# Key padding, the expert choice and the state's addition moved between engines in a gated-attention and mixture-of-experts kernel

## The chip, the core and the metric

The kernel runs on one core of a Trainium2 chip. Time is device microseconds of that core for one execution; a kernel's time is the median of several executions. Five engines run their own instruction streams in order and wait for each other by semaphores: TensorE (PE, with its weight loads as PEld), VectorE (DVE), ScalarE (ACT), GpSimd (POOL) and SyncE (SP), which issues most DMAs. Matrix products land in PSUM, which GpSimd cannot read.

## What is computed

For 4 batches and 8 heads of width 48, over 768 tokens, a gated linear attention keeps a 48x48 state per head; its rows then go to the one of 8 experts with the highest gate logit, and the expert's two-layer network gives the output.

```python
f = 1.0 / (1.0 + np.exp(-f_logit))
for t in range(S):
    state = f[:, :, t, :, None] * state + np.einsum('bhd,bhe->bhde', k[:, :, t], v[:, :, t])
    y[:, :, t] = np.einsum('bhd,bhde->bhe', q[:, :, t], state)
# x: y as 3072 rows of 384
expert_idx = np.argmax(x @ w_gate, axis=1)
# rows in order up to the capacity of their expert, then per expert e
h = np.maximum(disp[e] @ w1[e], 0.0)
out[i] = gate_w[i] * (h @ w2[e])[row of i]
```

## The kernel before

Attention runs over 24 chunks of 128 tokens of one batch, 6 chunks a batch, with the 8 heads as 4 pairs (NP). Chunk n's work is spread over several **slots**: slot n is one pass of `slot(n)` (L826), and its code is written out by hand in the order in which each engine gets its instructions; no scheduler moves them. A slot takes some 4.6 to 6.5 us; the 24 slots are followed by the experts' products, 150 to 325 us of the span, which PE fills alone.

On PE a slot holds, in this order: the scaled keys of chunk n turned to token rows (`keys_pe`, L451, into two buffers of the PSUM pool psT), the scores of chunk n+1 (`scores_pe`, L426, two buffers of psA), the padded keys and queries of chunk n+2 transposed (`kq_in`, L366, again two buffers of psT; that pool has two, so L366 can start only when the copies of the turned keys have left them), in odd slots decay gates (`f_in`, L366 into psF), the product of the old state with the queries (`inter`, L468), the new keys' and values' product (`update`, L488, into a psA buffer), in five slots the ranks of chosen rows (`rank_pe`, L675 to L682, where L679 is the first to read the choice), the attention rows of chunk n-1 (`rows_pe`, L543, psA) and the product of scores and values (`values`, L522). Then slot n+1 starts with its L451. The last chunk of a batch (slots 5, 11, 17, 23) has no L451 and no L488; the first (0, 6, 12, 18) no L468.

On ACT a slot copies the turned keys (`keys_out`, tile kn, L457, two copies), the attention output (yT, L534), the scores (AT, L432, two copies), in even slots takes the sigmoid of the gates (pf, L357), in some slots rounds a weight piece (`split_high`, L135), then copies the rows of chunk n-1 (L559) and their gate logits (tile parts, L569), and from slot 7 on (`PAD_ACT`, L78) pads keys and queries of chunk n+3 into tile kqp (`kq_pad`, L409). Before slot 7 GpSimd pads. On DVE: the choice of experts, the scaled keys and queries (kT and qT, L415), the state's sum U (`state`, L502, or L500, a copy, for a batch's first chunk), and two scans over the gates (`decay` L386 into Suf, `decay_back` L400 into Rq). On GpSimd: masks of the scores (L434), the next state S (`carry`, L508, which multiplies U by the decay), then a scatter of one chunk's rows to their experts' places in DRAM (`flush_scatter`, L326, one or two in a slot from slot 7), sums of gate logits (L577, L578) and parts of weight splits (L144).

The choice of experts for a group of chunks runs in three steps: `choose_sum` on GpSimd, `choose_max` (L583 to L586) at the end of that slot on DVE, and in the next slot `choose_first` (L591, L593), whose result, tile tally, the ranks on PE in the same slot read. These are slots 6, 10, 14, 17 and 20. SP's queue, in order: the keys and queries of chunk n+6 (L210), which overwrite what the padding has read and so wait for it, the gates (L216), the values (L205) and weight pieces (L122, L128).

Of the kernel before, what the change touches and what calls it, by code (L numbers as in the profile page):

```python
# [14 lines left out]
AF = mybir.ActivationFunctionType  # L15
ALU = mybir.AluOpType
# [13 lines left out]
def kernel(  # L30
# [12 lines left out]
    nc = tc.nc  # L43
    B, H, S, D = q.shape
# [9 lines left out]
    R = 64 + D  # L54
# [23 lines left out]
    PAD_ACT = 7  # L78
# [54 lines left out]
    def split_high(piece):  # L133
        raw, hi, lo = piece
        return nc.scalar.activation(hi, raw, AF.Copy)  # L135
# [82 lines left out]
    def loaded(nm, n):  # L218
        return loads[nm, n % NLOAD[nm]]
# [16 lines left out]
    Sb = []  # L236
# [115 lines left out]
    def sig(u):  # L352
        if u >= NT // 2:
            return
        cuts = (0, 64, P) if u == 0 else (0, P)
        for r0, r1 in zip(cuts, cuts[1:]):
            pace["ins"] = nc.scalar.activation(  # L357
                pf[u % 2][r0:r1, :, :, :D], loaded("f", u)[r0:r1].rearrange("t h j d -> t j h d"), AF.Sigmoid
            ).ins
# [43 lines left out]
    def kq_pad(n):  # L403
        if n < NT:
            src = loaded("kq", n).rearrange("t h j d -> t j h d")
            if n - 3 < PAD_ACT:
                nc.gpsimd.tensor_copy(kqp[n % 2][:, :, :, :D], src)
            else:
                nc.scalar.activation(kqp[n % 2][:, :, :, :D], src, AF.Copy)  # L409

    def kq_in(n):
        pts = transposes(*((psT.tile([P, NP, C], F32, name="psT"), kqp[n % 2], h) for h in range(2)))
        for nm, pt, by, made in (("kT", pts[0], Sufb[n % 2], kTs), ("qT", pts[1], Rqs.pop(n), qTs)):
            t = abuf.tile([P, NP, C], F32, name=nm, bufs=3)
            nc.vector.tensor_tensor(t[:R].rearrange("r p t -> r (p t)"), pt, by[:R], op=ALU.mult)  # L415
            made[n] = t
# [22 lines left out]
    def first(n):  # L439
        return n % CPB == 0  # L440

    def last(n):
        return n % CPB == CPB - 1
# [10 lines left out]
    def keys_out(n, pks):  # L454
        kn = abuf.tile([P, NP, R], F32, name="kn")
        for s, m in enumerate(MS):
            nc.scalar.activation(kn[:, :, 64 * s : 64 * s + m], pks[s][:, :, :m], AF.Copy)  # L457
        kns[n] = kn
# [37 lines left out]

    def state(n, pu):
        U = abuf.tile([P, NP, D], F32, name="U", bufs=1)
        if first(n):
            nc.vector.tensor_copy(U[:R], pu[:R])  # L500
        else:
            nc.vector.tensor_tensor(U[:R], pu[:R], Sb[n % 2][:R, :, :D], op=ALU.add)  # L502
        pus[n] = U

    def carry(n):
        if n in pus:
            U = pus.pop(n)
            nc.gpsimd.tensor_tensor(  # L508
                Sb[(n + 1) % 2][:R, :, :D],
                U[:R],  # L510
                pendall[:R, n + 1].unsqueeze(2).broadcast_to([R, NP, D]),
                op=ALU.mult,
            )
# [75 lines left out]
    def choose_first(g, m, w):  # L589
        wm = abuf.tile([P, m], F32, name="r_wm")  # L590
        nc.vector.tensor_reduce(out=wm, in_=w, axis=AX.X, op=ALU.max)  # L591
        oh = tallies[-1][:, 1 : m + 1]
        nc.vector.tensor_tensor(oh, w, wm.unsqueeze(2).broadcast_to([P, m, NE]), op=ALU.is_equal)  # L593
        chosen[g] = oh, m
# [171 lines left out]
    quarters, half = [0] * DT, []  # L766
# [59 lines left out]
    def slot(n):  # L826
        slot_now["n"] = n
        prev, cur, nxt = 0 <= n - 1 < NT, 0 <= n < NT, 0 <= n + 1 < NT
        kqn, fn = 0 <= n + 2 < NT, 0 <= n + 3 < NT
        tail = n - 1 >= NT - NCH  # L830
        keyed = cur and not last(n)
        done = ends.get(n - 1)
        if keyed and n:
            keys_out(n, keys_pe(n))
        if prev and not (cur and first(n)):
            y_out(n - 1)
        if nxt:
            pas = scores_pe(n + 1)
        if 0 < n < PAD_ACT:
            kq_pad(n + 3)  # L840
        if n == 3:
            nc.gpsimd.tensor_copy(ring[:, :, DM + NE : W], tokid[:, :RING].unsqueeze(2))
        while half:
            choose_first(*half.pop())
        for g in full:
            choose_sum(*g)
        if n == 1:
            f_in(4)
        if kqn:
            kq_in(n + 2)  # L850
        if n % 2 and fn and n not in (1, 9, 15):
            f_in(n + 3, n + 4)
        if nxt:
            scores_out(n + 1, pas)
        if n == 0:
            sig(2)
        if prev and cur and first(n):
            y_out(n - 1)
        if n % 2 == 0 and n > 0 and fn:
            sig((n + 4) // 2)  # L860
        if n in PIECE_SPLIT:
            split_high(pieces[PIECE_SPLIT.index(n)])
        loads_of(n)
        early_job(n, 0)
        if cur:
            inter(n)
        if n in (9, 15):
            f_in(n + 3, n + 4)
        early_job(n, 1)
        if keyed:  # L870
            pu = update(n)
        if split_at["n"] == n:
            pc = split_pe()
        ranks = [(g, chosen[g][1], rank(g, None)) for g in list(chosen) if not done or g != done[0]]
        if keyed:
            state(n, pu)
        if split_at["n"] == n:
            split_count(pc)
        ranked = [(g, m, pick(*job)) for g, m, job in ranks]
        if tail:  # L880
            for g, m, job in ranked:
                put(*job)
                queue.extend(range(g, g + m))
            ranked = []
        if keyed:
            carry(n)
        if n == 0:
            kq_pad(3)
            load("kq", 6)
        if nxt:  # L890
            for s in range(SCATTERS.get(n, 2)):
                flush_scatter()
        if fn:
            F = decay(n + 3)
        if prev:
            px = rows_pe(n - 1)
            if tail:
                rows_logits(n - 1, px)
                rows_copy(n - 1, px)
                chosen[n - 1] = choose_one(row_at(n - 1), abuf, tallies[-1][:, 1:2]), 1  # L900
            else:
                rows_copy(n - 1, px)
                rows_parts(n - 1, px)
        if fn and n >= PAD_ACT:
            kq_pad(n + 3)
            load("kq", n + 6)
        if n in QUARTERS:
            k, parts = QUARTERS[n]
            for part in range(parts):
                split_low(pieces[k], nc.gpsimd, PARTS, quarters[k])  # L910
                quarters[k] += 1
        if fn:
            decay_back(n + 3, F)
        for g, m, job in ranked:
            put(*job)
            queue.extend(range(g, g + m))
            if g + m == SPLIT:
                split_at["n"] = n + 1
        while full:
            g = full.pop()  # L920
            half.append((*g, choose_max(*g)))
        if prev and done and not tail:
            g, m = done
            if n - 1 >= NT - 2 * NCH:
                sum_parts(g, m)
                chosen[g] = choose(rows_at(g, m), m, abuf, tallies[-1][:, 1 : m + 1]), m
            else:
                full.append(done)
        if cur:
            values(n)  # L930
        if n % 2 == 0 and n and fn:
            load("f", (n + 4) // 2 + 2)
        if n == 1:
            f_in(5)
        if tail:
            early_job(n, 2)
            g, m = done
            place(*rank(g, psT))
            queue.extend(range(g, g + m))
            flush_scatter()  # L940
        else:
            early_job(n, 2)
        for k in pieces:
            if k >= DT and PIECE_SPLIT[k] == n:
                split_low(pieces[k], nc.vector)
        if n == 4:
            nc.gpsimd.tensor_copy(cap, cap_i[:, 0:1])
        if n == NT - 5:
            ins = nc.sync.dma_start(xg0, dispv[0, : T_FIRST[0]].rearrange("(k p) w -> p k w", p=P))
            tc.declare_no_dep(ins.ins, group="late", reason="later tokens of this expert go to rows of their own")  # L950
            after(ins, early_ins[0], "the rows of the early tokens")
        if n == NT - 3:
            checks.append(check_decay())
        if n == NT - 2:
            pc = psT.tile([P, 1], F32, name="psT")
            nc.tensor.matmul(pc, onesb[:R], checks[0][:R], start=True, stop=True)
            nc.vector.tensor_copy(bad_i, pc)
# [533 lines left out]
```

## Time and profile before

| | us |
|---|---|
| time, median of 3 executions | 373.35 (372.59 to 375.57) |
| the profiled execution | 375.17 |
| its span, from first to last instruction | 373.4 |
| PE busy | 362.1 |
| DVE, ACT, POOL busy | 247.8, 223.8, 166.5 |
| mean granted TensorE clock | 0.990 of full speed |

The profile is one execution. A matrix product's start is recorded, its end is modelled, so a busy PE may hide a wait inside a product's recorded time; the distance from one group's start to the next group's start shows it. A wait is named by the work that ended it. Idle time of an engine costs only where the engine that bounds the span waits for it.

### The profile page before, as it was taken

How to read it: one execution, taken by the hardware profiler on the slowest of the kernel's cores; microseconds unless marked ns; L12 is line 12 of the kernel's file. 1: busy time of each engine (PE TensorE's matmuls, PEld its weight loads, DVE VectorE, ACT ScalarE, POOL GpSimd, SP SyncE). 2: the span in 40 equal slices, each digit the busy share in tenths (PEclk: the TensorE clock that was granted, in tenths of full speed). 3: DMA queues.
4: the chain of work that ended last, by engine and by line, in shares of the span. 5: the costliest groups of instructions: out<-in, count | busy, mean ns of one | idle time of the engine just before them, and what ended most of it. 6: DMA issues, size and time to landing. Idle time of an engine off the chain costs nothing.

```text
span 373.4 us, 10082 instructions
## 1 busy us (share of the span) xinstructions
PE 362.1 (97%) x3895; PEld 340.8 (91%) x3895; DVE 247.8 (66%) x533; ACT 223.8 (60%) x458; POOL 166.5 (45%) x275
## 2 busy tenths in 40 slices
PE   8999999999899999999999999999999999999993
PEld 7999898888787889999899999999999999999993
DVE  4898988979687866753676296857757665570300
ACT  3356677877586763255477475759578586583310
POOL 6665556675757675235613702127117244144012
PEclk9999999999899999999999999999999999999997
DMA  8999999999997432476696979799797997721001
GB/s 153 187 177 224 205 207 227 256 214 226 213 227 164 130 114 105 133 237 204 191 239 188 286 196 242 212 187 319 169 204 247 172 208 253 129 94 52 14 23 40
DMA packets 111351, 67.86 MB, mean 182 GB/s; under 512 B 93646, under 2 KB 105844, under 8 KB 111296
## 3 DMA queue, kind: packets, MB, share of 16 engines
q1 hardware_dynamic: 107504, 57.09, 69.1%
q0 software_dynamic: 3520, 9.97, 7.7%
q8 instruction: 32, 0.52, 0.6%
q14 instruction: 23, 0.19, 0.2%
q10 hardware_dynamic: 272, 0.10, 0.1%
HBM read 49.46 MB, written 11.43 MB: 163 GB/s over the span
## 4 chain that ended last, share of the span: by engine, by line
PE 84%; issue 8%; ACT 3%; POOL 2%; DVE 1%; POOLq 1%; ACTq 0%
PE psM L1222 15%; PE psA L754 9%; PE psM L1015 9%; PE psT L754 9%; PE psM L754 7%; PE psA L426 6%; PE psY L522 6%; PE psA L543 5%; PE psT L366 4%; PE psY L468 3%; PE psA L488 3%; PE psT L451 3%; PE psF L366 2%; POOL out_dram L326 2%; PE psA L376 2%
## 5 line engine op out<-in xcount | busy, mean ns | idle before, releaser
L326 POOL DMA_INDIRECT out_dram<-yo,g_ti x30 | 31.3, 1042 | 55.6 <-ACT yo L1019 31.7
L434 POOL TENSOR_SCALAR_AFFINE_SELECT AT<-AT 128x512 f32<-128x512 f32 x48 | 29.4, 637 | 23.3 <-ACT AT L432 23.2
L1015 PE MATMUL psM<-w2h,hh 128*128 128x384 f32 (+2 forms) x112 | 37.5, 340 | 0.0
L1015 PE MATMUL psM<-w2l,hh 128*128 128x384 f32 (+2 forms) x112 | 37.3, 338 | 0.0
L1015 PE MATMUL psM<-w2h,hl 128*128 128x384 f32 (+2 forms) x112 | 37.2, 338 | 0.0
L135 ACT ACTIVATE w2h<-raw 128x768 fp32r<-128x768 f32 x32 | 27.0, 844 | 11.2 <-DMA raw<-in_moe_w_dram 11.2
L1222 PE MATMUL psM<-hh,w2h 128*128 128x440 f32 (+3 forms) x96 | 33.7, 351 | 0.0
L1222 PE MATMUL psM<-hh,w2l 128*128 128x440 f32 (+3 forms) x96 | 33.7, 351 | 0.0
L1222 PE MATMUL psM<-hl,w2h 128*128 128x440 f32 (+3 forms) x96 | 33.6, 350 | 0.0
L144 DVE TENSOR_TENSOR w2l<-raw,w2h 128x768 fp32r<-128x768 f32 x28 | 27.8, 994 | 7.7 <-ACT w2h L135 6.9
L386 DVE TENSOR_TENSOR_SCAN Suf<-psF,direv 112x511 f32<-112x511 f32 x24 | 29.1, 1212 | 4.5 <-PE psF L366 4.5
L432 ACT ACTIVATE AT<-psA 128x512 f32<-128x512 f32 x48 | 26.4, 612 | 8.9 <-PE psA L426 5.6
L1242 POOL COPY yo<-yq 128x384 uint16<-128x384 uint16 (+4 forms) x16 | 11.9, 790 | 40.1 <-DMA yq<-yp 38.2
L426 PE MATMUL psA<-qT,kT 48*128 48x128 f32 x384 | 29.4, 293 | 0.0
L400 DVE TENSOR_TENSOR_SCAN Rq<-psF,d 112x512 f32<-112x512 f32 x24 | 29.4, 1223 | 0.0
L326 POOL DMA_INDIRECT disp<-rows,ri x24 | 24.8, 1034 | 9.5 <-issue 4.3
L144 DVE TENSOR_TENSOR w1l<-raw,w1h 128x1024 fp32r<-128x1024 f32 x21 | 26.5, 1269 | 2.9 <-ACT w1h L135 2.6
L761 DVE SCALAR_TENSOR_TENSOR hl<-psA,hh 128x224 fp32r<-128x224 f32 (+8 forms) x26 | 14.2, 547 | 21.3 <-ACT hh L760 19.3
L559 ACT ACTIVATE rows<-psA 128x384 f32<-128x384 f32 x24 | 11.8, 491 | 26.0 <-PE psA L543 19.6
L522 PE MATMUL psY<-AT,ld_v 128*48 128x128 f32 (+1 forms) x384 | 26.9, 278 | 0.0
L426 PEld LDWEIGHTS psA<-qT,kT 48*128 48x128 f32 x384 | 25.8, 201 | 0.5 <-issue 0.5
L135 ACT ACTIVATE w1h<-raw 128x1024 fp32r<-128x1024 f32 x24 | 24.8, 1060 | 1.9 <-DMA raw<-in_moe_w_dram 1.9
(253 smaller groups left out, 1041.7 us busy)
## 6 DMA issues: line engine op xcount, KB each, us to landing
raw<-in_moe_w_dram SPq DMA_DIRECT2D x24, 512.0 KB
raw<-in_moe_w_dram SPq DMA_DIRECT2D x32, 384.0 KB
ld_kq<-in_k_dram SPq DMA_DIRECT2D x24, 192.0 KB
ld_kq<-in_q_dram SPq DMA_DIRECT2D x24, 192.0 KB
ld_v<-in_v_dram SPq DMA_DIRECT2D x24, 192.0 KB
ld_f<-in_f_logit_dram SPq DMA_DIRECT2D x11, 384.0 KB
xg<-disp SPq DMA_DIRECT2D x6, 589.5 KB
xg<-disp SPq DMA_DIRECT2D x3, 393.0 KB
```

The costliest lines, as they stand in the source:

```text
L135: return nc.scalar.activation(hi, raw, AF.Copy)
L144: engine.tensor_tensor(lo[cs], raw[cs], hi[cs].bitcast(F32), op=ALU.subtract)
L326: ins = nc.gpsimd.indirect_dma_start(out=dst, out_offset=bass.IndirectOffsetOnAxis(ap=idx, axis=0), in_=rows, in_offset=None, bounds_check ...
L386: nc.vector.tensor_tensor_scan(out=_view(Suf[:R], m - 1, [[-1, m]]), data0=_view(F, m, [[-1, m]]), data1=_view(direv[:R], m - 1, [[-1, m]] ...
L400: nc.vector.tensor_tensor_scan(out=Rq[:R], data0=F, data1=d1[:R], initial=0.0, op0=ALU.mult, op1=ALU.max)
L426: nc.tensor.matmul(pas[s][:, p], kTs[n][r, p], qTs[n][r, p], start=True, stop=True)
L432: nc.scalar.activation(AT[:, s], pas[s], AF.Copy)
L434: nc.gpsimd.affine_select(AT[:, s], AT[:, s], pattern=[[0, NP], [1, C]], compare_op=ALU.is_ge, fill=0.0, base=0, channel_multiplier=-1)
L522: nc.tensor.matmul(py[b][64 * g : 64 * g + m, a, :], vt[:, 2 * p + s, :m], AT[:, s, p, :], start=(first(n) and a == 0), stop=(a == NP // 2 ...
L754: nc.tensor.matmul(ph[:, :T], a[:, c, fs], x[:, c, :T], start=(n == 0), stop=(n == 3 * DT - 1))
L1015: nc.tensor.matmul(py[:n], x[:, ks], a[:, ft], start=(ft == 0 and m == 0), stop=(ft == FT - 1 and m == 2))
L1222: nc.tensor.matmul(pys[c][:, :T], a[:, ft, cs], x[:, :T], start=(ft == 0 and n == 0), stop=(ft == FT - 1 and n == 2))
```

## The change

Four edits. From slot 7 the state's product leaves PSUM by a plain copy on ACT, and GpSimd adds the old state in front of the multiplication that it has done so far (for a batch's first chunk there is nothing to add); DVE no longer touches U in these slots. The padding on ACT moves from behind the rows' and logits' copies to the place behind the sigmoid, ahead of the weight rounding, of the new state copy and of the rows. The issue of the loads of chunk n+6 moves with it, so that on SP's queue they now stand ahead of that slot's values and weight pieces. In every slot that has one, `choose_first` moves behind the scaled keys and queries.

```diff
     def state(n, pu):
         U = abuf.tile([P, NP, D], F32, name="U", bufs=1)
-        if first(n):
+        if n >= PAD_ACT:
+            nc.scalar.activation(U[:R], pu[:R], AF.Copy)
+        elif first(n):
             nc.vector.tensor_copy(U[:R], pu[:R])
         else:
             nc.vector.tensor_tensor(U[:R], pu[:R], Sb[n % 2][:R, :, :D], op=ALU.add)
...
             U = pus.pop(n)
+            if n >= PAD_ACT and not first(n):
+                nc.gpsimd.tensor_tensor(U[:R], U[:R], Sb[n % 2][:R, :, :D], op=ALU.add)
             nc.gpsimd.tensor_tensor(
...
-        while half:
-            choose_first(*half.pop())
         for g in full:
             choose_sum(*g)
         if n == 1:
             f_in(4)
         if kqn:
             kq_in(n + 2)
+        while half:
+            choose_first(*half.pop())
...
             sig((n + 4) // 2)
+        if fn and n >= PAD_ACT:
+            kq_pad(n + 3)
+            load("kq", n + 6)
         if n in PIECE_SPLIT:
             split_high(pieces[PIECE_SPLIT.index(n)])
         loads_of(n)
...
-        if fn and n >= PAD_ACT:
-            kq_pad(n + 3)
-            load("kq", n + 6)
         if n in QUARTERS:
```

DVE in slot 10, from the scan in front of the choice, before (r_m, r_w and r_wm are steps of the choice, tally its result):

```order
L400 SCALAR_TENSOR_TENSOR Rq<-psF,d_145 112x512
L583 TENSOR_REDUCE r_m<-rows 128x4
L585 TENSOR_TENSOR r_w<-rows,r_m 128x32
L586 TENSOR_TENSOR r_w<-r_w,desc 128x32
L591 TENSOR_REDUCE r_wm<-r_w 128x4
L593 TENSOR_TENSOR tally<-r_w,r_wm 128x32
L415 TENSOR_TENSOR kT<-psT,Suf_141 112x512
L415 TENSOR_TENSOR qT<-psT,Rq 112x512
L502 TENSOR_TENSOR U<-psA,S_147 112x192
```

The same place of the changed kernel (its line numbers are 2 to 4 higher from L500 on):

```order
L400 SCALAR_TENSOR_TENSOR Rq<-psF,d_145 112x512
L587 TENSOR_REDUCE r_m<-rows 128x4
L589 TENSOR_TENSOR r_w<-rows,r_m 128x32
L590 TENSOR_TENSOR r_w<-r_w,desc 128x32
L415 TENSOR_TENSOR kT<-psT,Suf_141 112x512
L415 TENSOR_TENSOR qT<-psT,Rq 112x512
L595 TENSOR_REDUCE r_wm<-r_w 128x4
L597 TENSOR_TENSOR tally<-r_w,r_wm 128x32
L646 TENSOR_TENSOR r_sel<-psA,tally 128x4x8
```

The last two steps of the choice moved behind kT and qT, and U's addition is gone.

ACT in slot 8, from the output copies to the next slot's copies of the turned keys, before:

```order
L534 ACTIVATE yT<-psY 112x2x128 x2
L432 ACTIVATE AT<-psA 128x512 x2
L357 ACTIVATE pf_118<-ld_f_100 128x16x48
L559 ACTIVATE rows<-psA 128x384
L569 ACTIVATE parts<-psA 128x32
L409 ACTIVATE kqp_124<-ld_kq_105 128x16x48
L457 ACTIVATE kn<-psT 128x4x64
```

The same place of the changed kernel:

```order
L538 ACTIVATE yT<-psY 112x2x128 x2
L432 ACTIVATE AT<-psA 128x512 x2
L357 ACTIVATE pf_118<-ld_f_100 128x16x48
L409 ACTIVATE kqp_124<-ld_kq_105 128x16x48
L500 ACTIVATE U<-psA 112x192
L563 ACTIVATE rows<-psA 128x384
L573 ACTIVATE parts<-psA 128x32
L457 ACTIVATE kn<-psT 128x4x64
```

The padding moved ahead of the rows, and the copy of U came in between.

GpSimd in slot 8, from the masks to the sums of logits, before:

```order
L434 AFFINE_SELECT AT<-AT 128x512 x2
L508 TENSOR_TENSOR S_149<-U,pendall 112x4x48
L326 DMA disp<-rows,ri 32256x393
L577 TENSOR_TENSOR parts<-parts 128x4x16
L578 TENSOR_TENSOR rows<-parts 128x4x8
```

The same place of the changed kernel:

```order
L434 AFFINE_SELECT AT<-AT 128x512 x2
L511 TENSOR_TENSOR U<-U,S_147 112x192
L512 TENSOR_TENSOR S_149<-U,pendall 112x4x48
L326 DMA disp<-rows,ri 32256x393
L581 TENSOR_TENSOR parts<-parts 128x4x16
L582 TENSOR_TENSOR rows<-parts 128x4x8
```

The addition stands between the masks and the multiplication, and the scatter behind both.

## Rows read from the trace of the kernel before

**Rows 1.** The page: busy time, share of the span and instructions of each engine.

```profile
PE 362.1 (97%) x3895; PEld 340.8 (91%) x3895; DVE 247.8 (66%) x533; ACT 223.8 (60%) x458; POOL 166.5 (45%) x275
```

**Rows 2.** Timeline, slots 8 to 9: start, duration, engine, line, tiles, idle before.

```profile
53.84 1.19 POOL L326 DMA_INDIRECT disp<-rows,ri  x1 [0.38 <-issue]
54.22 1.12 PE L426 MATMUL psA<-qT,kT 48*128 48x128 f32 x16
54.49 0.60 ACT L457 ACTIVATE kn<-psT 128x256 f32<-128x256 f32 x2
55.73 0.67 PE L468 MATMUL psY<-qT,S 48*64 48x128 f32 x16
56.46 0.89 ACT L357 ACTIVATE pf<-ld_f 128x768 f32<-128x768 f32 x1
57.12 0.36 DVE L502 TENSOR_TENSOR U<-psA,S 112x192 f32<-112x192 f32 x1
57.56 0.51 POOL L508 TENSOR_TENSOR S<-U,pendall 112x192 f32<-112x192 f32 x1
58.16 0.19 ACT L569 ACTIVATE parts<-psA 128x32 f32<-128x32 f32 x1
58.30 1.01 POOL L326 DMA_INDIRECT disp<-rows,ri  x1 [0.23 <-issue]
60.56 0.67 PE L468 MATMUL psY<-qT,S 48*64 48x128 f32 x16
```

**Rows 3.** Timeline, slot 10, the same columns.

```profile
63.86 1.01 POOL L326 DMA_INDIRECT disp<-rows,ri  x1 [0.22 <-issue]
64.40 1.12 PE L426 MATMUL psA<-qT,kT 48*128 48x128 f32 x16
64.79 1.36 SPq L210 DMA_DIRECT2D ld_kq<-in_k_dram  x1
65.26 0.60 ACT L457 ACTIVATE kn<-psT 128x256 f32<-128x256 f32 x2 [0.60 <-PE psT L451]
65.70 0.88 PE L366 MATMUL psT<-ident,kqp 64*112 64x64 f32 x16 [0.18 <-ACT kn L457]
66.44 0.19 DVE L593 TENSOR_TENSOR tally<-r_w,r_wm 128x32 bf16<-128x32 f32 x1
66.51 0.67 PE L468 MATMUL psY<-qT,S 48*64 48x128 f32 x16
66.57 0.69 DVE L415 TENSOR_TENSOR kT<-psT,Suf 112x512 f32<-112x512 f32 x1
67.18 0.68 DVE L415 TENSOR_TENSOR qT<-psT,Rq 112x512 f32<-112x512 f32 x1
67.77 0.22 PE L679 MATMUL psA<-tally,onesb 128*128 128x24 bf16 x3
```

**Rows 4.** Groups by form, 50 to 132 us: count, busy, mean ns, idle before.

```profile
L409 ACT ACTIVATE kqp<-ld_kq 128x768 f32<-128x768 f32 x14 | 11.9, 847 | 0.0
L559 ACT ACTIVATE rows<-psA 128x384 f32<-128x384 f32 x15 | 7.4, 491 | 14.7 <-PE psA L543 14.5
L457 ACT ACTIVATE kn<-psT 128x256 f32<-128x256 f32 x13 | 5.0, 384 | 3.7 <-PE psT L451 2.7 <-PE psA L426 1.0
L457 ACT ACTIVATE kn<-psT 128x192 f32<-128x192 f32 x13 | 4.3, 328 | 0.1
...
L415 DVE TENSOR_TENSOR kT<-psT,Suf 112x512 f32<-112x512 f32 x15 | 10.4, 691 | 6.3 <-PE psT L366 6.3
```

**Rows 5.** Timeline, slot 6, the columns of rows 2.

```profile
46.04 0.69 DVE L415 TENSOR_TENSOR kT<-psT,Suf 112x512 f32<-112x512 f32 x1
46.96 0.22 PE L679 MATMUL psA<-tally,onesb 128*128 128x24 bf16 x3
```

**Rows 6.** Busy by stretch: PE, PEld, DVE, ACT, POOL, granted clock, DMA share, GB/s.

```profile
96.50:100.00 3.50, 2.54 (x53) 1.77 (x49) 1.91 (x3) 2.86 (x7) 3.42 (x8) 0.99 1.21 216
100.00:103.40 3.40, 3.40 (x45) 3.34 (x41) 2.62 (x5) 1.31 (x3) 2.02 (x4) 0.51 1.07 202
```

## The prediction

> **What bounds the kernel now.** I read the page first. PE is busy for 362.1 us of the span and no other engine is busy for more than 66% [rows 1]. So PE's own row of work is the bound, and of the other engines only what PE waits for counts. Behind slot 23 PE alone is at work, so that whatever a slot gains or loses reaches the end one for one.
>
> The second view is the timeline of single slots, with the question where PE waits. A product's end is modelled, so I go by starts. In slot 8, L426 starts at 54.22 and L468 at 55.73, 1.51 apart [rows 2]. In slot 10 the same two stand at 64.40 and 66.51, 2.11 apart [rows 3]: PE did no more work, and .60 were lost. Between them L366 started "behind ACT kn", and kn itself had waited .60 for L451 [rows 3]. Over slots 8 to 21 the groups by form put this at 2.7 + 1.0 = 3.7 us, all of it on the first of kn's two copies [rows 4]. Nothing stands in front of the padding's own 14 instructions (idle 0.0) and 14.5 us of idle stand in front of the 15 row copies [rows 4]: ACT has room there.
>
> The third is what ran while kn was late. The view names L451, but in slot 10 PE was through L451 when it began L426, at 64.40, ACT was free from 64.66 (65.26 less its idle .60), and kn began only at 65.26, .86 after L426; in slot 8 it began .27 after [rows 2, 3]. A scatter on GpSimd lay across slot 10's gap, from 63.86 to 64.87 [rows 3]. I read this as L451's signal coming late while the scatter runs, .39 after its end. That is an inference, and one row speaks against it: in slot 8 a scatter lay there too, from 53.84 to 55.03, and kn came on time [rows 2]. The change moves the scatter as well as the padding.
>
> The fourth is the busy time by stretch. In 96.5 to 100 us PE is busy for 2.54 of 3.50, and the next 3.4 us run at a granted clock of 0.51, the 1.2 GHz level, although PE is busy in all of them; ahead it was 0.99 [rows 6]. At half speed 3.40 us do the work of 1.7, so this fall costs 1.7 us at most; I take 1.5, since part of it may be waits inside the recorded times. Waits of about 1 us in one stretch thus can cost more than their length.
>
> **The change part by part.** The sum is against the profiled execution, 375.17, which is 1.8 above the median 373.35 of the runs.
>
> *Padding ahead of the rows.* 14 paddings of 847 ns [rows 4] go from behind the logits' copies, in front of the next slot's kn, into the wait of 14.5 us in front of the row copies, about 1.0 each. In that place they cost nothing as long as the row copies do not come later than their products allow. In even slots the sigmoid, .89, stands ahead (slot 8: 56.46 to 57.35 [rows 2]); padding to 58.20, U's copy to 58.53, rows and logits (.49 + .19) to 59.21, where before the logits ended at 58.35 and the padding about 59.2. So kn comes no later, but the logits are copied up to .9 later, which keep a psA buffer from the next L426, 54.22 + about 4.5; I put .2 for seven even slots together. If the cover were gone wholly, each slot would lose up to .85. What is gained: the kn waits, 3.7 us, if all of them go. The bounds are 0 (they come from the scatter, which stays) and 3.7; I count the whole and book separately what comes back.
>
> *Loads of chunk n+6.* Two DMA issues a slot go ahead of the values and weight pieces on SP's queue. No padding waited for its loads (0.0 [rows 4]), which come three slots ahead; values move back by two issues. The slots of 4.6 us and more hide that: 0. If the cover were gone, a slot would wait for its values for what the two issues take on the queue, at 1.36 for the keys [rows 3] some 2.7 us, once.
>
> *U on ACT, the addition on GpSimd.* DVE loses 12 x .36 = 4.3 us [rows 2] that PE did not wait for. ACT gets 14 copies of 112x192 from PSUM, nearest to the 328 ns of kn's 128x192 [rows 4], between that and the .49 of the row copy. GpSimd gets 12 additions; the trace of before has none, so its bounds are the DVE's .36 for the same addition and 1.01, the longest row of GpSimd in that slot; the nearest row is its own multiplication of the same size, .51 [rows 2], which I take. In slot 8 U was ready at 57.48 and S at 58.07, and L468 of slot 9 reads S at 60.56 [rows 2]: 2.5 us of slack. Now U is ready at 58.53, added at 59.1, S at 59.65: .9 is left. On the path: 0. Were the cover gone, each slot would pay what exceeds .9. The Trainium skill (GPSIMD Engine Reference, section 4.1, Engine selection) advises against this: an elementwise addition belongs on VectorE, since GpSimd is about twice as slow with two inputs. Here DVE's .36 against GpSimd's .51 for two inputs is 1.4 times; by the page's factor the estimate would be .72, S .2 later, and the sum the same.
>
> *What comes back: the scatter.* It stands behind the multiplication on GpSimd. Before, it began .23 after it; now the multiplication ends about .5 later in odd slots and 1.6 later in even ones, so in even slots the scatter of 1.01 moves from 58.30 to about 59.9, that is from the start of slot 9's L451 to the time of kn's second copy and L366 behind it. If the scatter holds signals back, the wait is not removed but goes to other slots: I put .4 (its lag behind the scatter's end in slot 10) for slots 8, 14, 16 and 20, 1.6 us; .9 for the two scatters each that stand in slots 18 and 19, which now end later; and .5 in slots 10 and 17, where L366 coming .6 earlier finds DVE still at the scan and the first three steps of the choice, so that kT gains less than L366. Together 3.0; bounds 0 and, with .4 in all 13 slots, 5.2.
>
> *The choice behind kT and qT.* PE never waits for kT by itself; DVE's kT waited 6.3 us for PE's L366 [rows 4]. So kT coming earlier gains nothing. But L679 on PE reads tally. In slot 10 before, kT began at 66.57 and L679 at 67.77, with tally ready at 66.63. Now tally is ready behind kT (.69), qT (.68) and L591 and L593 (.41 from the first one's start to the other's end), with their overlap of .08 taken off: 1.70 after kT's start, 68.27, so .50 late [rows 3]. In slot 6: 46.04 + 1.70 = 47.74 against 46.96, .78 late [rows 5]. Slots 14, 17 and 20 are built as 10. In sum .78 + 4 x .5 = 2.8 us of new PE wait, with rows L543, values L522 and the next slot queued behind it. Bounds: 0 where PE is late anyway, 4.0 with .8 in each.
>
> Sum: -3.7 + 3.0 + 2.8 + .2 = +2.3 us, so 377.5 for an execution like the profiled one, and **375.7** for the median.
>
> **The rivals.** *Faster.* The scatter holds nothing back (it was the padding, or the late place is free of signals), so the kn waits go for good, and with the one in slot 16 the fall of the clock, 1.5. Then -3.7 - 1.5 + 2.8 + .2 = -2.2: **371**; and 368 if the choice is hidden too, at its bound of 0. For it: the scatter of slot 8 that delayed nothing. Against it: in slot 10 ACT had been free for .60 when kn began, so that the padding was not what it waited for. Chance .25, of which .15 ends beyond 1%.
>
> *The clock falls more often.* The new waits for tally of .5 to .8 fall in slots that have a scatter besides; one stretch with 1.0 idle in 3.5 was followed by 3.4 us at 1.2 GHz [rows 6]. Two more falls at 1.6 give 375.7 + 3.2 = **379**. For it: slots 10, 14 and 17 may then have two waits each. Against it: waits of 3.7 us were there before [rows 4], and the mean granted clock of 0.990 over 373.4 us leaves room for a loss of 3.7 us in all, some two falls. It decides from two more on. Chance .23.
>
> *S comes late.* If the addition takes over 1.4 instead of .51, the slack of .9 is spent, and L468 waits in 12 slots; with the ACT copy late too, .3 each: 375.7 + 3.6 = **379**. For it: GpSimd now does two operations and a scatter in a row. Against it: GpSimd is busy for 45% only [rows 1]. Chance .10.
>
> **How the numbers follow.** The forecast, .42: its own range is 374 to 377.5. The faster rival .25, the clock .23, S late .10. About 1% of the time, 3.7 us, is what a measurement of this kernel can tell from no change, so faster means below 369.6 and slower above 377.1. Faster: .15 from its rival. Slower: .20 of the clock's .23, .08 of S late's .10 and .06 from the upper end of the forecast, .34 together. The rest, .51, is the same. The range runs from 369.0, between the two ends of the faster rival, to 380.0, one more us than both slower rivals; I leave about .10 out on either side.
>
> **What would show it.** Right, in the profile of after: a gap of .5 to .8 ahead of L679's group in slots 6, 10, 14, 17 and 20, with tally (DVE) as what ended it; no wait ahead of kn's first copy anywhere, but a wait of some .4 ahead of the second, or of L366, in even slots, with a scatter lying across it; S ready ahead of L468 everywhere; GpSimd's additions at .4 to .7; row copies without idle time in front in even slots. Wrong: L679 not waiting (then the choice was free, and 2.8 go); no waits with the scatter in its late place (then the padding was the cause, and 3.0 go); a granted clock of .5 in a stretch of slots 6 to 20 in which before had .99, which is the second rival; L468 waiting for S; or weight pieces landing late behind the moved loads.

## The result, and the profile after

| | before | changed |
|---|---|---|
| time, median | 374.10 us (4 executions) | 379.01 us (378.12 to 381.11, 4 executions) |
| ratio | | 1.0139, 95% interval 1.0101 to 1.0177 |
| the profiled execution, its span | 375.17, 373.4 | 381.11, 379.4 |

The change costs 1.4%, some 5 us. In a later measurement of the same two kernels, with 35 and 12 executions, the medians were 373.47 and 375.33 and the ratio 1.0077 (1.0044 to 1.0111). (Ratios leave out executions over 1.5% above the fastest of their kernel and are not the quotient of the medians, which take all.) Together: about 1% slower, with 375.7 forecast and 380 the upper end of the range.

The page of the changed kernel, busy time of each engine (before: [rows 1]):

```profile
PE 357.3 (94%) x3895; PEld 335.4 (88%) x3895; DVE 245.9 (65%) x519; ACT 228.8 (60%) x472; POOL 176.4 (46%) x287
```

PE does the same 3895 products, but stands idle more. What PE waited for between 40 and 200 us, in the table of waits of the changed kernel (total us, times, longest):

```profile
PE psA L683 <- DVE tally L597: 3.9, 5, 1.0
PE psA L758 <- DVE hl L765: 2.0, 1, 2.0
PE psF L366 <- issue: 1.6, 2, 1.0
...
PE psT L366 <- issue: 0.9, 1, 0.9
```

The same table of before has no row above 1.2 us. The new first row is the moved choice: L683 (L679 in before) waits for the tally in all five slots that have one. Slot 6 in the timeline of the changed kernel (start, us, engine, line, tiles, idle before); before stands in [rows 5]:

```profile
46.31 0.69 DVE L415 TENSOR_TENSOR kT<-psT,Suf 112x512 f32<-112x512 f32 x1 [0.37 <-PE psT L366]
...
47.09 1.23 POOL L434 TENSOR_SCALAR_AFFINE_SELECT AT<-AT 128x512 f32<-128x512 f32 x2
...
47.73 0.62 DVE L597 TENSOR_TENSOR tally<-r_w,r_wm 128x32 bf16<-128x32 f32 x1
...
48.41 0.22 PE L683 MATMUL psA<-tally,onesb 128*128 128x24 bf16 x3 [1.02 <-DVE tally L597]
```

And slot 10, to be laid beside [rows 3]:

```profile
67.29 1.12 PE L426 MATMUL psA<-qT,kT 48*128 48x128 f32 x16
67.40 1.01 POOL L326 DMA_INDIRECT disp<-rows,ri  x1 [0.22 <-issue]
67.56 0.60 ACT L457 ACTIVATE kn<-psT 128x256 f32<-128x256 f32 x2 [0.73 <-PE psT L451]
...
68.25 0.62 PE L366 MATMUL psT<-ident,kqp 64*112 64x64 f32 x16
...
68.96 0.69 DVE L415 TENSOR_TENSOR kT<-psT,Suf 112x512 f32<-112x512 f32 x1 [0.82 <-PE psT L366]
...
70.37 0.33 DVE L597 TENSOR_TENSOR tally<-r_w,r_wm 128x32 bf16<-128x32 f32 x1
...
70.76 0.22 PE L683 MATMUL psA<-tally,onesb 128*128 128x24 bf16 x3 [0.53 <-DVE tally L597]
```

kn now starts .27 after L426, as in slot 8 of before, instead of .86: the wait that the change took away is gone. ACT's .73 in front of kn costs nothing, for the padding that filled it has moved. But PE loses at L683 what it won at L366. By starts, L683 comes 1.18, .68, .67, .93 and 1.19 us later behind the rank product ahead of it than L679 does in before, in slots 6, 10, 14, 17 and 20: 4.65 in all. (The expectations below have .70, .90, .70 and 1.27 for the last four.)

The row on hl, the low part of an expert's hidden rows, which DVE makes, is a stretch behind the attention. Busy times there (us of the stretch; PE, PEld, DVE, ACT, POOL; granted clock; DMA share; GB/s):

```profile
190.00:192.30 2.30, 0.32 (x3) 0.13 (x2) 1.08 (x6) 1.94 (x4) 1.59 (x2) 1.00 0.96 375
192.30:196.00 3.70, 3.70 (x10) 3.10 (x11) 3.67 (x8) 3.62 (x8) 0.11 (x1) 0.54 1.13 278
```

PE stands for 2.0 us and then runs most of 3.7 us at a granted clock of .54, near the 1.2 GHz level. Of the 6.0 us between the two profiled spans, by the starts of L426, .3 lie ahead of slot 6, 2.3 between slots 6 and 22 and 3.5 behind. Whether this stall belongs to the change is asked below.

### The profile page after: what moved, and what is told of

Read it like the earlier page. It is cut to its first block, busy times and chain, and to the rows that moved or that the text cites. A ratio compares the mean times of both kernels' runs of the same rounds, so it can differ in the third digit from the quotient of the medians.

```text
span 379.4 us, 10089 instructions
## 1 busy us (share of the span) xinstructions
PE 357.3 (94%) x3895; PEld 335.4 (88%) x3895; DVE 245.9 (65%) x519; ACT 228.8 (60%) x472; POOL 176.4 (46%) x287
## 4 chain that ended last, share of the span: by engine, by line
PE 72%; issue 9%; DMA 6%; POOL 4%; SPq 3%; DVE 3%; ACT 2%; POOLq 1%; ACTq 0%; DVEq 0%
PE psM L1226 14%; PE psA L758 9%; PE psM L1019 9%; PE psT L758 8%; PE psM L758 6%; PE psA L426 5%; DMA ld_kq<-in_q_dram 5%; PE psA L547 4%; PE psY L526 4%; PE psY L468 2%; PE psT L366 2%; POOL out_dram L326 2%; PE psA L488 2%; PE psF L758 2%; PE psT L451 2%
## 5 line engine op out<-in xcount | busy, mean ns | idle before, releaser
L1246 POOL COPY yo<-yq 128x384 uint16<-128x384 uint16 (+4 forms) x16 | 12.7, 839 | 39.4 <-DMA yq<-yp 37.8
L426 PE MATMUL psA<-qT,kT 48*128 48x128 f32 x384 | 28.4, 281 | 0.7 <-ACT parts L573 0.7
L526 PE MATMUL psY<-AT,ld_v 128*48 128x128 f32 (+1 forms) x384 | 26.1, 273 | 0.0
L426 PEld LDWEIGHTS psA<-qT,kT 48*128 48x128 f32 x384 | 24.7, 189 | 1.5 <-ACT parts L573 1.1
L415 DVE TENSOR_TENSOR kT<-psT,Suf 112x512 f32<-112x512 f32 x24 | 16.5, 688 | 14.2 <-PE psT L366 13.4
```

The source lines that it names most:

```text
L426: nc.tensor.matmul(pas[s][:, p], kTs[n][r, p], qTs[n][r, p], start=True, stop=True)
L526: nc.tensor.matmul(py[b][64 * g : 64 * g + m, a, :], vt[:, 2 * p + s, :m], AT[:, s, p, :], start=(first(n) and a == 0), stop=(a == NP // 2 ...
```

## The experiments

The first four ran on one chip with 29 executions of before (median 374.41), the next four later on the same chip with 35 (373.47), the last four on another chip with 26 (374.97). Each is compared with its own group.

**The choice alone.** The kernel before, with one edit:

```diff
-        while half:
-            choose_first(*half.pop())
...
             kq_in(n + 2)
+        while half:
+            choose_first(*half.pop())
```

> The kernel before with one edit only: choose_first behind kT and qT. Theory (the choice carries the loss): in the profile of after PE stands for tally in slots 6, 10, 14, 17 and 20, and the distance between the two kernels grows there by 1.18, .70, .90, .70 and 1.27, so this edit alone costs 4.7 us: about 378.8 against 374.1. Rival (the loss is the late state and scatter, and the wait for tally only takes the place of waits that come anyway): 375 to 376.

Measured: 379.03, ratio 1.0106 (1.0058 to 1.0155). This edit alone costs as much as the whole change. PE's waits in its profile, 40 to 200 us:

```profile
PE psA L679 <- DVE tally L593: 2.9, 5, 1.0
...
PE psT L366 <- ACT kn L457: 0.6, 3, 0.3
```

kn's waits stayed, since neither padding nor scatter moved. In slot 20 the wait for the tally was also followed by a fall of the clock, in the busy times by stretch (the columns are those of the stretch on hl):

```profile
124.00:126.50 2.50, 1.98 (x39) 1.81 (x41) 2.08 (x7) 1.10 (x2) 1.64 (x4) 0.91 0.21 34
126.50:130.00 3.50, 3.50 (x44) 3.15 (x42) 3.16 (x7) 2.35 (x7) 1.54 (x4) 0.58 0.53 149
```

So waits of 2.9 us grew to more: by starts, PE fell back 3.6 us at L679 and another 1.4 between slot 20's L522 and slot 21's L366. That the wait of slot 20 caused the fall is not shown: the longer one of slot 6 (1.0) had none behind it.

**The padding alone.** `kq_pad(n + 3)` and `load("kq", n + 6)` behind the sigmoid, nothing else.

> The kernel before with one edit only: the padding and the loads of chunk n+6 ahead of the rows. Theory (a scatter on GpSimd holds the signal for kn back, and this edit does not move the scatter): kn's waits of 3.7 us stay, 374 as before. Rival (the padding was what made kn late): they go, 370, or 369 with the clock's fall in slot 16.

Measured: 375.62, ratio 1.0026 (.9995 to 1.0057): no gain. kn's lateness stayed. Slot 14 in its timeline:

```profile
88.50 1.01 POOL L326 DMA_INDIRECT disp<-rows,ri  x1 [0.22 <-issue]
...
88.75 0.46 PE L451 MATMUL psT<-ident,kT 64*128 64x64 f32 x8
...
89.88 0.60 ACT L457 ACTIVATE kn<-psT 128x256 f32<-128x256 f32 x2 [1.31 <-PE psT L451]
...
90.32 0.88 PE L366 MATMUL psT<-ident,kqp 64*112 64x64 f32 x16 [0.17 <-ACT kn L457]
```

ACT stood free for 1.31 us, with the padding long done, and kn still began only .37 after the scatter's end. The padding was not the cause. New was a wait of L488 for its values, .67 and a further .62 in slot 10, after which the granted clock was .53 from 71 to 74.5 us.

**The state alone.** U by ACT, the addition by GpSimd, nothing else.

> The kernel before with one edit only: U copied on ACT and the old state added on GpSimd. Theory (the scatter holds signals back wherever it lies): the scatter comes .5 to .9 later, kn's waits of 3.7 us shrink but a wait ahead of L366 of about .4 to 1.0 comes in some slots; 373 to 375. Rival (S or U late is what costs): L468 waits for S, or L488 for the psA buffer that U leaves, in most slots, 377 or more.

Measured: 372.50, ratio .9939 (.9911 to .9967). It is the only one of all kernels here, the changed one included, whose interval lies below 1. Slot 14 in its timeline:

```profile
85.05 0.46 PE L451 MATMUL psT<-ident,kT 64*128 64x64 f32 x8
...
85.44 1.01 POOL L326 DMA_INDIRECT disp<-rows,ri  x1 [0.22 <-issue]
85.55 0.60 ACT L457 ACTIVATE kn<-psT 128x256 f32<-128x256 f32 x2
...
86.30 0.61 PE L366 MATMUL psT<-ident,kqp 64*112 64x64 f32 x16
```

The same place of before:

```profile
84.05 1.01 POOL L326 DMA_INDIRECT disp<-rows,ri  x1 [0.22 <-issue]
84.30 0.46 PE L451 MATMUL psT<-ident,kT 64*128 64x64 f32 x8
...
85.48 0.61 ACT L457 ACTIVATE kn<-psT 128x256 f32<-128x256 f32 x2 [0.63 <-PE psT L451]
```

GpSimd's addition has pushed the scatter from .25 ahead of L451 to .39 behind it, and kn starts .50 after L451 instead of 1.18. The scatter runs in both when L451 ends, but L451's modelled end falls .07 behind the scatter's start instead of .70. All of kn's idle time between 50 and 132 us was .7 us, against 3.7 [rows 4], and it stood in slot 7, which has no scatter ahead of it; in slots 8 to 22 there was none. The waits at L366 that the theory expected in exchange did not come, but for one of .6 on DVE's Rq.

**Padding and state, the choice in its old place.**

> The changed kernel with choose_first back in its old place. Theory (the choice carries the loss): 379.0 less 4.7, 374.3, with no wait for tally. Rival (late state and scatter): 377 or more, with waits of about 1.0 at L366 in slots 8, 9 and 19 as in after.

Measured: 373.94, ratio .9997 (.9967 to 1.0027). The changed kernel without the choice's move is as fast as before, as the theory had it. The waits at L366 in slots 8 and 9 were not there, the one in slot 19 was, 1.0.

**The scatter ahead of the multiplication**, in the kernel before:

```diff
+        if nxt:
+            for s in range(SCATTERS.get(n, 2)):
+                flush_scatter()
         if keyed:
             carry(n)
-        if nxt:
-            for s in range(SCATTERS.get(n, 2)):
-                flush_scatter()
```

> The kernel before with one edit: the scatter stands ahead of the state's multiplication on GpSimd instead of behind it, some .7 earlier; padding, U and choice as before. Theory (a scatter that lies across L451 holds kn's signal back; the state's move helped alone because it pushed the scatter past it): kn's waits of 3.7 us go, and with them the clock's fall in slot 16, so 371 to 372 against 374.4. Rival (the state's move helped because U is taken off DVE or comes at another time): kn's waits stay, 374.4; S comes later by the scatter's 1.0 and has 2.5 of slack.

Measured: median 372.12, but a ratio of 1.0014 (.9981 to 1.0047): no difference that can be told, where the theory had 2 to 3 us. The waits did go as foretold. The group of kn in its profile (50 to 132 us: count, busy, mean ns, idle before):

```profile
L457 ACT ACTIVATE kn<-psT 128x256 f32<-128x256 f32 x13 | 5.0, 382 | 0.0
```

From 3.7 to 0.0, with only the scatter moved. In this profile slot 6's L426 to slot 22's took 80.95 us, against 86.21 in before, of which the fall of the clock in slot 16 is at most 1.7 [rows 6]; what is left, 3.5 or more, fits kn's waits. Behind slot 22 PE lost 1.69 at 183 us to the stall on hl.

**The loads back.** Padding and state, but the loads of chunk n+6 issued at the slot's end.

> Padding and state moved, choice in its old place, but the loads of chunk n+6 issued at the slot's end as before instead of ahead of the values. Theory (the loads' new place makes the values late: L488 waited .7 and .6 for ld_v in slot 10 with the padding moved alone, .5 with padding and state): no such wait, 372.5, like the state moved alone. Rival (the padding in its new place costs, by pushing U, the rows and the logits back): 374, as with the loads moved.

Measured: 373.12, ratio 1.0032 (.9986 to 1.0078), not to be told from the kernel with the loads moved (.9997), so that it decides for neither expectation. The wait for values was gone from the profile, and others stood there: L547 .7 and L426 .5.

**The changed kernel again.**

> The changed kernel once more, unaltered. The stall of 2.3 us at 190 us in its first profile, with the rows' load of the next expert late, is counted to the change by one reading: then it stands in this profile too. By the other it is the chance of one execution, as the weight loads land: then it is missing or smaller, and the time of this profile is 377 to 379 instead of 381.1. Median 378.7 to 379 by both.

Measured: 375.33, ratio 1.0077 (1.0044 to 1.0111). PE's waits in this profile, 40 to 200 us:

```profile
PE psA L683 <- DVE tally L597: 2.1, 4, 0.8
PE psA L488 <- DMA ld_v<-in_v_dram: 1.8, 2, 1.2
PE psF L366 <- DVE Rq L400: 1.0, 1, 1.0
```

The stall on hl is missing, so it is no part of the change. It stood in the profiles of seven of the twelve experiments, of padding alone and of the early scatter among them, at 1.0 to 2.5 us. The median fell below what both readings had said; the first measurement's other three executions (378.1 to 379.1) have no trace, and why they were slower stays open. The waits for the values came in addition here.

**The ranks behind the rows**, in the changed kernel, so that PE works while the tally is made:

```diff
-        ranks = [(g, chosen[g][1], rank(g, None)) for g in list(chosen) if not done or g != done[0]]
...
                 rows_parts(n - 1, px)
+                ranked = [(g, m, pick(*job)) for g, m, job in [(g, chosen[g][1], rank(g, None)) for g in due]]
```

> The changed kernel with the ranks on PE moved behind the products of the rows (L547), so that PE has .76 us of other work while the tally is made. Theory (the choice costs what PE stands for the tally): of the waits 1.2, .7, .7, .7 and 1.2 only .4 each in slots 6 and 20 are left, the loss shrinks by 3.8, 375.2 against 379.0. Rival (the choice's new place costs in another way, by pushing DVE's later work, the scans and the copy of U's buffer): 378 to 379 as before, with the wait for the tally gone all the same.

Measured: 374.68, ratio 1.0083 (1.0045 to 1.0120), as the changed kernel in the same group. The rival was right about the time. The wait for the tally had gone, and this stood in its place:

```profile
PE psA L679 <- ACT U L500: 1.6, 3, 0.6
```

The ranks take the PSUM buffer that U leaves, and U's copy on ACT, behind the padding, is late: one wait turned into another.

**The choice between kT and qT**, in the kernel before, ahead of qT's product inside `kq_in`.

> The kernel before with choose_first moved behind kT only, ahead of qT. Theory (the choice costs only what the tally comes later than PE reads it): the tally is ready .69 + .41 = 1.10 after kT's start, PE read it 1.20 after it in slot 10 and .92 in slot 6, so .0 to .2 a slot, at most .5 in sum: the same time as before within .5. Rival (each step that the choice moves down the queue costs, by what stands behind it on DVE): about half of what the move behind both cost alone (4.6), 2.3 more than before.

Measured: 375.65 against 374.97, ratio 1.0041 (1.0018 to 1.0065). PE waited .7 us for the tally in two slots instead of 2.9 in five. The cost sits between the two expectations, nearer to the theory in the waits; the rest of the .4% no row accounts for. The tally took .26 to .64 us in this kernel, not the .19 of the expectation.

**State and early scatter together**, in the kernel before.

> The kernel before with the state's edit alone and the scatter ahead of GpSimd's addition. Theory (both edits did one thing, to take the scatter off L451's signal): no more than either alone, 1 to 2 us below before, with no wait for kn left. Rival (the state's edit has a gain of its own, DVE without U): 3 us below before.

Measured: 375.94 against 374.97, ratio 1.0024 (1.0003 to 1.0046). Both were wrong. Slot 8 on GpSimd and ACT:

```profile
52.95 1.20 POOL L326 DMA_INDIRECT disp<-rows,ri  x1 [0.20 <-issue]
...
54.31 0.49 ACT L563 ACTIVATE rows<-psA 128x384 f32<-128x384 f32 x1 [1.05 <-PE psA L547]
...
54.77 0.84 ACT L409 ACTIVATE kqp<-ld_kq 128x768 f32<-128x768 f32 x1
...
55.51 0.61 ACT L457 ACTIVATE kn<-psT 128x256 f32<-128x256 f32 x2
```

The scatter now lies across the products of the rows, the row copy begins .16 after the scatter's end, the padding stands behind it on ACT, and kn behind the padding, 1.17 after L451. Which signal the scatter holds is a matter of its place, and here the late one reaches kn through ACT's queue.

**The changed kernel with the early scatter.**

> The changed kernel with the scatter ahead of GpSimd's addition instead of behind the multiplication. Theory (the scatter in its later place holds PE back at L366, .9 to 1.0 in slots 8 and 19): these go, 2 less than the changed kernel, that is 1 to 2 above before, with the waits for the tally left. Rival (those waits are not the scatter's): as the changed kernel, 3 to 4 above before.

Measured: 378.55 against 374.97, ratio 1.0098 (1.0070 to 1.0125): the rival's time. The waits on L366 marked "issue" were gone, as the theory said, but the waits for the tally came to 4.1, 2.6 of it in slot 17:

```profile
103.11 0.51 POOL L512 TENSOR_TENSOR S<-U,pendall 112x192 f32<-112x192 f32 x1
103.12 1.83 DVE L590 TENSOR_TENSOR r_w<-r_w,desc 128x24 f32<-128x24 f32 x1
...
103.56 0.18 POOL L562 COPY rows<-tokid 128x1 f32<-128x1 f32 x1
...
103.70 1.22 POOL L434 TENSOR_SCALAR_AFFINE_SELECT AT<-AT 128x512 f32<-128x512 f32 x2
...
107.07 0.19 PE L683 MATMUL psA<-tally,onesb 128*128 128x16 bf16 x2 [2.59 <-DVE tally L597]
```

A DVE instruction of the choice that takes .19 (median of its five) took 1.83 here: GpSimd worked without a gap from 103.11 to 104.92, and the DVE instruction ended at 104.95.

**Plain work in the scatter's old place**: the early scatter, and eight memsets on GpSimd where it had stood.

> The kernel of the early scatter with eight small memsets on GpSimd (of a spare tile, about 1 us in all) where the scatter stood before, behind the multiplication. Theory (it is the scatter's own making of descriptors that holds signals back, not GpSimd being busy): kn's wait stays 0.0 as with the early scatter alone, and the time 1 to 2 below before. Rival (any work of GpSimd across L451 does it, by its order or its use of memory): the waits of about 3.7 us return, and the time is that of before.

Measured: 377.73 against 374.97, ratio 1.0069 (1.0044 to 1.0094); 2.6 us of PE's waits were now in front of L468, which reads S. (The view names a memset, but S stands ahead of the memsets on GpSimd, behind the early scatters.) The time answers neither side. A slot in which only the memsets lie across L451 does:

```profile
94.48 0.46 PE L451 MATMUL psT<-ident,kT 64*128 64x64 f32 x8
...
94.65 1.35 POOL L893 MEMSET spare<- 128x24 f32 x8
...
95.04 0.60 ACT L457 ACTIVATE kn<-psT 128x256 f32<-128x256 f32 x2
```

kn came on time, .56 after L451, and so it did in slot 21, the other one in which only memsets lie there and ACT was free. GpSimd being busy does not hold the signal back. The 0.0 of the theory did not come back: kn was late by .61, .51, .44 and 1.18 us in slots 13, 14, 19 and 22, where a scatter again ran when L451 ended.

## Why the prediction was right in its main step, and where its terms were off

**kn's waits, -3.7.** Right in the cause, with a limit that the prediction did not see; the price is borne out by starts, not by the times. Of 182 first copies of kn in slots 8 to 22 of the fourteen profiles, 88 had a scatter running when L451 ended (by its modelled end), and 33 of them began over .15 us later than L451 and ACT allowed; of the other 94 one did. So a scatter is needed, whether the padding moved (padding alone: late) or not (early scatter and state alone: none late), and plain work does not do it. But it is not enough, and slot 8 was no lone exception: in before, kn was on time under a scatter in slots 8, 9, 20 and 22 and late in 10, 13, 14, 15, 16 and 19. What counts is where in the scatter L451 ends: within .6 us of the scatter's start 5 of 44 were late, all in kernels with the early scatter, later in it 28 of 44. In the changed kernel a scatter still ran there in seven slots, begun only .03 to .56 earlier, and kn was on time in all. Between .69 and .98 both outcomes occur; what decides there stays open.

As time, the state alone gained .6%, 2.3 us, and the early scatter nothing that can be told, with all 3.7 gone in both. One step of the first paragraph failed here: "Behind slot 23 PE alone is at work, so that whatever a slot gains or loses reaches the end one for one." From slot 22's L426 to the end the fourteen profiles took 241.8 to 246.2 us, and in nine of them PE stood there for hl, .2 to 2.5 us. That spread is as large as the whole change, so a gain of 3 us in the slots can be lost to it.

**The choice, +2.8.** The step that decided, with the right sign and cause, and rather undersized. The waits were 2.9 in the choice alone, 3.9 and 2.1 in the two profiles of the changed kernel; as time the edit cost 1.06%, 4.0 us, with 2.2 to 5.8 as its interval, in which 2.8 still lies; in its profiled execution 1.4 was the clock. The term that was mis-sized is the tally's own .19, taken from [rows 3], where GpSimd was idle. Behind kT and qT it falls under GpSimd's masks and took .18 to .62 (median .33) in the first profile of the changed kernel, .18 to .45 (median .21) in the second, which also had the smaller waits. In slot 6 of the first it began at 47.73 and ended at 48.35, .03 after the mask that ran beside it; slots 10 and 14 show the same. The Trainium skill (GPSIMD Engine Reference, section 1, Specifications) says that GpSimd's paths to SBUF are shared with VectorE, with contention for VectorE instructions that have two SBUF inputs; the tally and L590 have two, kT and qT take one of theirs from PSUM and stay at .69 and .68. These rows agree.

**What comes back, +3.0.** The place was wrong, and the size is measured only together with kn's waits and the row copies: -3.7 + 3.0 + .2 = -.5 was forecast, and padding and state together came to -.1 us (-1.2 to 1.0). The later scatter did not hold up kn's second copy: in the changed kernel kn was on time in every slot. L366 waited .86 in slot 8 with a scatter across it, in one of the two profiles of the changed kernel only. What did come back is U's lateness. In slot 18 of the changed kernel:

```profile
112.93 0.86 ACT L409 ACTIVATE kqp<-ld_kq 128x768 f32<-128x768 f32 x1
...
113.66 0.35 ACT L500 ACTIVATE U<-psA 112x192 f32<-112x192 f32 x1
...
114.05 0.16 DVE L670 TENSOR_SCALAR csplit<-psA 128x1 f32<-128x1 f32 x1 [1.67 <-ACT U L500]
...
117.15 0.66 PE L366 MATMUL psF<-ident,pf 64*112 64x64 f32 x15 [1.01 <-issue]
```

U, behind sigmoid and padding, holds DVE's csplit up, the scans come behind that, and in slot 19 L366 waits 1.0 for the gates' PSUM buffer; the second profile names the scan Rq as what ended it. I had priced U's slack to S alone and not looked at what else waits behind it.

**The loads, 0.** Off in the waits, and not to be told in the times. Of six profiles with the loads moved, five show L488 waiting for its values, .5 to 1.8 us in sum (the changed kernel's first does not); of the seven with the loads in their place, and of before, none does. The bound of 2.7 held.

**U, S and the addition, 0.** Right for S: the addition took .595 against .51, and no wait of L468 in the changed kernel was ended by S.

**The fall of the clock in slot 16.** It was counted into no sum, but the faster rival rested on it. It was absent from the choice alone, whose kn waited there as before, so that the fall was one execution's. Falls of the clock came in other places in three other profiles, each behind a stretch with .5 to 2 us of PE idle; other stretches of that size had none behind them (slot 6 of the changed kernel, 1.0).

**The rivals.** The faster one fell with the choice. S late did not come. The clock's rival was half right: one fall in the choice alone, none in the second profile of the changed kernel; the one at 192 us in the first came behind the stall on hl, not behind a wait for the tally. The outcome, 1.4% and .8% slower, lies on the border between "same" and "slower", above the .6% that 375.7 stood for.

**The sum.** Measured apart, the choice cost 4.0 and the rest -.1, against +2.8 and -.5 forecast, so the split was right. That the second measurement, +2.9 us, lies so near to the forecast +2.3 is in part luck: the tally was priced too low, and what came back came from other places than the sum had it, late values and a late U.

## What to carry to other kernels

A step that is moved down an in-order queue costs what its reader elsewhere then waits, and its own duration must be taken at its new place, beside what the other engines do there. A stall that is removed by shifting a neighbour is worth nothing until one knows which signal the neighbour meets next. A stretch behind the change that is taken to pass gains on one for one has to be timed, too, in several profiles. When several edits are made at once, measure each alone: here one gained .6%, the padding beside it gave that gain back, and a move of two lines lost 1%.

## What the runs showed of the hardware

A GpSimd scatter with indices, about 1.0 us long, can hold back signals of other engines. kn, behind L451, was late in 33 of 88 cases in which a scatter ran when L451 ended, and in 1 of 94 others; 31 of the late ones began .31 to .69 us after the scatter's end, two 1.05 and 1.06 after it, with a second scatter on its heels. A row copy behind L547 began .16 after it. Eight memsets of 1.35 us in the same place did not hold kn back in the two slots that show it.

The trace's semaphore records fit this. In before, between 50 and 132 us, the 15 longest stretches in which no update of any semaphore, by an engine or a DMA, is recorded (.51 to .78 us; the longest away from scatters is .46) all lie at a scatter, and 14 of them begin .61 to .80 us after its start and outlast it by .07 to .61. By its modelled end, L451 of slot 10 ended at 64.57, inside such a stretch (64.50 to 65.15), that of slot 8 at 54.39, ahead of it (54.49 to 55.10). So it is a part of the scatter, not the whole, that holds signals; why is not shown.

A VectorE step of the choice with two SBUF inputs took .18 to .20 us in all 84 cases of the fourteen profiles with GpSimd idle, and in 75 of 77 that began under a scatter. Where it began under another GpSimd instruction with more than .16 us left, it ended .03 to .05 us after that one in 44 of 46 cases (.62 in slot 6 of the changed kernel), and in two it stood behind the following ones as well (1.05 and 1.83).
